# Issuing the second maxima product of a step ahead of the second piece of P times V (attention with shared keys and a gated MLP)

## The chip, the cores and the metric

One core of a Trainium2 chip runs one launch. The metric is the device time in microseconds of that launch. A profile comes from one execution, and its times count from that execution's first instruction. The engines are PE (TensorE; its weight loads are listed as PEld), DVE (VectorE), ACT (ScalarE), POOL (GpSimd) and SP, whose queue issues DMAs.

## The reference, cut to what matters

```python
mod = (silu(c) @ w_mod).reshape(1, 6, 1, 512)           # sa, ca, ga, sb, cb, gb
h = layernorm(x) * (1 + ca) + sa                        # x: 2048 x 512
q = (h @ wq) as 32 heads of 16;  k = h @ wk;  v = h @ wv   # one k and one v for all heads
p = softmax(q k^T / 4)                                  # per head 2048 x 2048
x = x + ga * ((p @ v) @ wo)
h = layernorm(x) * (1 + cb) + sb
x = x + gb * (((h @ w_gate) * (h @ w_up)) @ w_down)     # 1792 wide
```

The softmax needs, for every query and head, the maximum over the 2048 keys. The kernel forms the scores twice: once to take the maxima, and once, with the maximum subtracted by extra rows of the product, for the exponentials.

## The kernel before, in words

The 2048 queries are cut into 4 blocks of 512, the 32 heads into 8 groups of 4. A block with a head group is one of `NU` = 32 rounds, and a round has `NSTEP` = 32 steps: 16 key tiles of 128 keys (`kt`), two steps each (`p`). In one step the main loop (L1162 to L1208) issues, in this order:

- `max_half(a, 0, 2)`, the **first maxima product**: `max_mm` (L557) multiplies 128 queries of one head of a later round by 512 keys into a bank `mx` of PSUM, as four PE matmuls that each fill 32 of the 128 output partitions (`quarters`, L474), and has DVE reduce the bank to 128 maxima (L566). There are `NMX` = 2 such banks, so a product waits for the reduce of the product two before it, which is the same product of the step before.
- `pv(*who, 0)`, the **first piece of P times V** (L604): the exponentials of an earlier key tile times the values, 256 of the 512 queries, four heads. These are float32 matmuls; each shows as two PE instructions, so a piece is two sets of four.
- `qk_exp(u, kt, 0, a)`, the first **score product** (L596), four matmuls into a bank `sc`, and its exponential on ACT (L602) into a buffer `P`.
- `pv(*who, 1)`, the second piece of P times V, the other 256 queries.
- `drain_mids()`: evacuations put off from an earlier step.
- `max_half(a, 1, 2)`, the **second maxima product**, with its reduce.
- `qk_exp(u, kt, 1, a)`, the second score product and its exponential.

The maxima and score products of a step read rows 64a to 64a + 63 of the PE array, with a = `p`, and P times V reads the other 64 rows. The two row halves change places with every step. The maxima run 38 steps (`LEAD`) ahead of the exponentials; the first 38 steps of maxima are issued before the main loop, and the last 38 steps of the loop have none.

What is left of a step on PE goes to **fill work**: the query projections of later blocks, and the output projection, the gate, up and down products of the block before. A planner (`pace`, L1056; `fill_gap`, L1077) works out from counts of steps, at build time, how many units each step takes, up to `BURST` = 3. A unit (one turn of the loops in `duo`, L485) is eight matmuls, four on each row half, for two output tiles side by side. When a pair of tiles is complete, the first is evacuated at once, and the second by a function put into `mids`, which `drain_mids` (L1023) calls in the next step. On DVE that concerns the output projection (L703) and the down product (L814); the copies after the up product are ACT's (L796). The second tile's bank is given back for scores three steps after that (L507).

`max_half` (L1029) counts the maxima steps. With its second product in a step with a = 1 it also issues, once in a round (at `QPRE` = 20 of the round's 32), six DMAs on SP that load the queries of the next round (`load_q`, L546), and at the end of a round the last reduce (L572). A wait on PE stands at the head of an instruction, and the instructions behind it wait too. Schedules are written out by hand: each engine gets its instructions in the order in which this code emits them.

Of the kernel before, what the change touches and what calls it, by code (L numbers as in the profile page):

```python
# [54 lines left out]
def adaln_mqa_glu_kernel(ctx: ExitStack, tc: tile.TileContext, x_in, wq_in, wk_in, wv_in, wo_in,  # L55
# [14 lines left out]
    def ps_sc():  # L70

        spare["n"] += 1
        if spare["scores"] and spare["n"] % (NSC + 1) == 0:
            return psum.tile([128, 512], F32, name="sc", tag="spare", bufs=1)
        return psum.tile([128, 512], F32, name="sc", tag="sc", bufs=NSC)
# [398 lines left out]
    def quarters(p, left, right, start=True, stop=True):  # L474
        return [nc.tensor.matmul(p[c:c + CW, :], left[:, c:c + CW], right, start=start, stop=stop)  # L475
                for c in range(0, 128, CW)]
# [69 lines left out]
    def load_q(u):  # L546
        b, g = divmod(u, UB)
        d = qd[b, g // 2].rearrange("(h e) l n -> e h l n", e=16)
        s = sst[u % 3]
        h0 = 4 * (g % 2)  # L550
        for a in range(2):
            for r, hl in ((0, 0), (1, 0), (2, 1)):
                nc.sync.dma_start(s[64 * a + 16 * r:64 * a + 16 * r + 16, :, :], d[:, h0 + a:h0 + a + 3:2, hl, :])
# [3 lines left out]
    def max_mm(u, i, a):  # L557
        kc, r = divmod(i, 8)
        p, t = divmod(r, 4)
        s = sst[u % 3]  # L560
        if i == 0 and a == 0:
            mparts[u] = work.tile([128, 2, 2, 4, 4], F32, name="mpart")
        m = ps_mx()
        quarters(m, s[64 * a:64 * a + 48, p, t * 128:(t + 1) * 128],
                 kst[64 * a:64 * a + 48, kc * 512:(kc + 1) * 512])
        nc.vector.tensor_reduce(mparts[u][:, a, p, t, kc:kc + 1], m, axis=AX.X, op=OP.max)  # L566
# [3 lines left out]
    def max_fin(u):  # L570
        mms[u] = work.tile([128, 2, 8], F32, name="mm")
        nc.vector.tensor_reduce(mms[u], mparts[u].rearrange("p a q t k -> p a (q t) k"), axis=AX.X, op=OP.max)  # L572

    def max_rows(u):
        def f():
            p = psum.tile([16, 128], F32, name="mxt", tag="mx", bufs=NMX)
            mms[u, "p"] = p
            nc.tensor.transpose(p, mms[u].rearrange("p a c -> p (a c)"), ident)

        def g():  # L580
            p = mms[u, "p"]
            mt = [work.tile([16, 128], F16, name=f"mt{hl}") for hl in range(2)]
            nc.scalar.activation(mt[0], p, AF.Copy, scale=1.0 / 32.0)
            nc.vector.scalar_tensor_tensor(mt[1], p, 1.0 / 32.0, mt[0], op0=OP.mult, op1=OP.subtract)
            s = sst[u % 3]
            for hl in range(2):
                nc.sync.dma_start(s[48 + hl:113 + hl:64, :, :], mt[hl])
        return [(100, f, g)]
# [7 lines left out]
    def qk_exp(u, kt, p, a):  # L596
        s = sst[u % 3]
        if (u, kt, a) not in ptl:
            ptl[u, kt, a] = work.tile([128, 2, D], F32, name="P", tag="P", bufs=NP)
        t = ps_sc()  # L600
        quarters(t, kst[64 * a:64 * a + 50, kt * 128:(kt + 1) * 128], s[64 * a:64 * a + 50, p, :])
        nc.scalar.activation(ptl[u, kt, a][:, p, :], t, AF.Exp)  # L602

    def pv(u, kt, r, part=None):  # L604
        if u < 0:
            return
        if kt == 0 and not part:
            pvb[u, r] = psum.tile([128, 512], F32, name="pv", tag=("pv", "pvb")[r], bufs=1)
        ks = slice(64 * r, 64 * r + 64)
        w = 512 // PARTS  # L610
        for c in range(PARTS) if part is None else (part,):
            for j in range(4):
                p, a = divmod(j, 2)
                nc.tensor.matmul(pvb[u, r][32 * j:32 * j + 32, c * w:(c + 1) * w], vst[ks, kt, :],  # L614
                                 ptl[u, kt, a][ks, p, c * w:(c + 1) * w], start=(kt == 0 and c == 0),
                                 stop=(kt == KT - 1 and c == PARTS - 1), skip_group_check=True)
# [3 lines left out]
    def pv_lower(u):  # L620
        evt[u] = work.tile([128, BT], F32, name="ev", tag="ev", bufs=3)
        nc.scalar.activation(evt[u], pvb[u, 0], AF.Copy, scale=evs)  # L622

    def pv_out(u):
        b, g = divmod(u, UB)
        ev = evt[u]
        nc.vector.scalar_tensor_tensor(ev, pvb[u, 1], evs, ev, op0=OP.mult, op1=OP.add)  # L627
        if g % 2 == 0:
            oc[b, g // 2] = work.tile([128, BT], F32, name="oc", tag="oc", bufs=2)
            rsum[b, g // 2] = dram.tile([8, BT], F32, name=f"rs{b}_{g // 2}")  # L630
        h = 4 * (g % 2)
        for j in range(4):
            r = 16 * (h + j)
            nc.sync.dma_start(oc[b, g // 2][r:r + 16, :], ev[32 * j:32 * j + 16, :])
        nc.sync.dma_start(rsum[b, g // 2][h:h + 4, :], ev[16:128:32, :])
# [378 lines left out]
    def drain_posts():  # L1014
        todo = posts[:]
        posts.clear()
        if tick[0] is not None:
            tick[0] += 1
            todo += timers.pop(tick[0], [])
        for f in todo:  # L1020
            f()

    def drain_mids():  # L1023
        todo = mids[:]
        mids.clear()
        for f in todo:
            f()

    def max_half(a, j=0, n=1):  # L1029
        u, i = divmod(mstep[0] + j, NSTEP)  # L1030
        if a == 1 and j == n - 1:
            mstep[0] += n
        if u >= NU:
            return
        max_mm(u, i, a)
        if a == 1 and u + 1 < NU and i == (QPRE if u else QPRE0):
            load_q(u + 1)
        if i == NSTEP - 1 and a == 1:
            max_fin(u)
            (_, f, g), = max_rows(u)  # L1040
            later[mstep[0] + 1] = (f, g)
# [25 lines left out]
    def open_gate(step):  # L1067
        if not fill or (fill[0][1] == "duo" and step < cur["wait"]):
            return False
        if fill[0][1] == "duo" and NU * NSTEP - step < 2 * -(-fill[0][2][0].n // BURST) + 2:  # L1070
            return False
        gate = fill[0][0]
        if gate[0] is None:
            gate[0] = step + gate[1]
        return gate[0] <= step
# [86 lines left out]
    for u in range(NU):  # L1162
        b, g = divmod(u, UB)
        if u == 1:
            side.extend(dlist)
        for i in range(NSTEP):
            step = u * NSTEP + i
            kt, p = divmod(i, 2)
            drain_posts()
            spare["scores"] = not spare["held"] and cur["gen"] is None and not (fill and fill[0][1] == "duo" and open_gate(step))  # L1170
            a = p
            if p == 1:
                who = (u, kt - 1, 0) if kt else (u - 1, KT - 1, 0)
                if u and not kt:
                    posts.append(lambda u=u: pv_lower(u - 1))
            else:
                who = (u, kt - 2, 1) if kt > 1 else (u - 1, KT - 2 + kt, 1)
                if u and kt == 1:
                    posts.append(lambda u=u: pv_out(u - 1))
            max_half(a, 0, 2)  # L1180
            pv(*who, 0)
            qk_exp(u, kt, 0, a)
            pv(*who, 1)
            drain_mids()
            max_half(a, 1, 2)
            qk_exp(u, kt, 1, a)
            if p == 1:
                late_max()
            if fill or cur["gen"]:
                credit[0] = min(credit[0] + pace(step) / 2, 6.0)  # L1190
                if credit[0] >= 1.0:
                    fill_gap(step)
            side_step(step)
            if u > 0 and g % 2 == 0 and i in (5, 9, 15):
                if i == 5:
                    nrm = normalise((u - 1) // UB, ((u - 1) % UB) // 2)
                nrm[(5, 9, 15).index(i)]()
            if i == 16 and u > 0 and g == 0:
                ln = ln2_work(b - 1)
                due = (b + 1) * UB * NSTEP + (DUE if b < NB - 1 else LAST_DUE)  # L1200
                gate = [step + 4, 0]
                for two in twos(wo_work(b - 1)):
                    fill.append((gate, "duo", two, due))
                for gap, it in zip((TR_GAP, 0, 0, 0), ln):
                    fill.append(([None, gap], "solo", it, due))
                gate = [None, 0]
                for two in ffn_twos(b - 1):
                    fill.append((gate, "duo", two, due))  # L1208
# [72 lines left out]
```

## Time and profile before

| | |
|---|---|
| median of 3 runs | 1770.66 us (1768.67 to 1771.16) |
| the profiled execution | 1768.31 us, span 1766.5 us |
| busy: PE, DVE, ACT, POOL | 1697.3, 1438.7, 1258.7, 562.8 us |
| exponentials, L602 | 2048 of 599 ns, 1133.9 us |
| P times V, L614 | 16384 of 379 ns (they overlap), 1089.4 us |
| reduces of the maxima, L566 | 2048 of 686 ns, 1325.0 us |
| granted PE clock, mean | 0.995 |

The PE matmuls are pipelined, and their ends are modelled. A line of the timeline gives the start in microseconds, the time from the first start to the last end of the merged instructions, the engine, the line of code, the operation, output and inputs, the shapes and the count; in brackets the idle time ahead of it, and what ended that. Such a releaser is inferred from semaphores. The row of a window gives the bounds, its length, and then for the chosen instructions their busy time and count; the last three numbers are the granted PE clock, the share of the DMA engines and their GB/s.

### The profile page before, as it was taken

What the parts mean: (1) busy time and instruction counts of PE and PEld (TensorE: products, weight loads), DVE (VectorE), ACT (ScalarE), POOL (GpSimd) and SP (SyncE); (2) the same over time, 40 slices, a digit from 0 to 9 for tenths busy, and PEclk for the clock granted to TensorE, in tenths of its full rate; (3) what the DMA queues carried; (4) which work ended last, traced back from release to release, by engine and by line L of the source; (5) the groups of instructions that cost most, each with busy time, mean ns of one, the idle gap of its engine ahead of it and who ended that gap; (6) DMA issues with size and microseconds to landing.
All of it is one profiled execution on the core that took longest, in us unless ns stands there. A gap on an engine that the chain in (4) does not pass through costs nothing. (4 is left out here: it accounts for less than half of the span.)

```text
span 1766.5 us, 102784 instructions
## 1 busy us (share of the span) xinstructions
PE 1697.3 (96%) x47395; PEld 1062.5 (60%) x47395; DVE 1438.7 (81%) x2353; ACT 1258.7 (71%) x2319; POOL 562.8 (32%) x788
## 2 busy tenths in 40 slices
PE   6899999999999999999999999999999999999999
PEld 3345555555556666776656766677656666754444
DVE  7899999999998888888999888899999998922210
ACT  3478888878877777777777777777788887883110
POOL 5714454537567852210032222100032121221130
PEclk9999999999999999999999999999999999999999
DMA  5212222212222210000100000000100000001000
GB/s 195 101 31 81 61 81 63 83 42 84 77 75 68 62 27 20 6 18 24 43 23 19 13 18 14 8 18 23 49 17 19 12 19 12 14 7 41 19 0 24
DMA packets 49179, 71.09 MB, mean 40 GB/s; under 512 B 15270, under 2 KB 29418, under 8 KB 48748
## 3 DMA queue, kind: packets, MB, share of 16 engines
q1 hardware_dynamic: 47164, 64.33, 12.2%
q8 instruction: 370, 6.06, 1.5%
q14 instruction: 61, 0.50, 0.1%
q10 hardware_dynamic: 1584, 0.20, 0.1%
HBM read 51.12 MB, written 8.92 MB: 34 GB/s over the span
## 5 line engine op out<-in xcount | busy, mean ns | idle before, releaser
L566 DVE TENSOR_REDUCE mpart<-mx 128x1 f32<-128x512 f32 x2048 | 1325.0, 686 | 123.8 <-PE mx L475 46.4
L602 ACT ACTIVATE P<-sc 128x512 f32<-128x512 f32 x2048 | 1133.9, 599 | 301.0 <-PE sc L475 194.0
L614 PE MATMUL pv<-P,vst 64*32 64x256 f32 x16384 | 1089.4, 379 | 0.8 <-ACT ev L622 0.7
L475 PE MATMUL mx<-kst,sst 48*32 48x512 f16 x8192 | 815.9, 383 | 36.1 <-DVE mpart L566 28.1
L475 PE MATMUL sc<-sst,kst 50*32 50x512 f16 x8192 | 824.9, 379 | 8.4 <-ACT P L602 6.8
L614 PEld LDWEIGHTS pv<-P,vst 64*32 64x32 f32 x16384 | 486.1, 106 | 93.5 <-issue 3.2
L475 PEld LDWEIGHTS <-sst 48*32 48x32 f16 x8192 | 340.0, 90 | 295.5 <-issue 222.1
L475 PEld LDWEIGHTS <-kst 50*32 50x32 f16 x8192 | 284.1, 91 | 78.5 <-issue 50.5
L475 PE MATMUL misc<-h2T,wg 64*32 64x512 f16 x4032 | 297.5, 376 | 1.1 <-issue 1.1
L475 PE MATMUL misc<-h2T,wu 64*32 64x512 f16 x4032 | 297.6, 376 | 0.0
L797 POOL TENSOR_TENSOR gf<-gf,g 128x512 f32<-128x512 f32 x42 | 53.6, 1276 | 346.5 <-ACT gf L796 346.5
L475 PEld LDWEIGHTS <-wu 64*32 64x32 f16 x4032 | 115.8, 92 | 30.2 <-issue 1.6
L475 PEld LDWEIGHTS <-wg 64*32 64x32 f16 x4032 | 115.3, 92 | 19.1 <-issue 2.6
L475 PE MATMUL misc<-wd,glu 64*32 64x512 f16 x2688 | 121.6, 376 | 0.0
L475 PE MATMUL misc<-h,wq 64*32 64x512 f16 x1536 | 100.6, 377 | 2.1 <-ACT qf L532 2.1
L499 POOL MEMSET token<- 1x1 f32 x43 | 3.8, 88 | 283.8 <-PE misc L475 242.4
L789 ACT ACTIVATE g<-misc 128x512 f32<-128x512 f32 x56 | 33.6, 600 | 76.6 <-PE misc L522 75.5
L522 PE MATMUL misc<-wd,glu 128*128 128x512 f16 x336 | 73.2, 379 | 0.0
L475 PEld LDWEIGHTS <-glu 64*32 64x32 f16 x2688 | 60.0, 92 | 17.7 <-issue 1.3
L801 POOL TENSOR_TENSOR glu<-gf,glu 128x512 f16<-128x512 f32 x56 | 65.1, 1163 | 4.7
L799 DVE TENSOR_TENSOR gf<-misc,g 128x512 f32<-128x512 f32 x14 | 9.7, 692 | 62.9 <-PE misc L522 62.9
L627 DVE SCALAR_TENSOR_TENSOR ev<-pv,evs,ev 128x512 f32<-128x512 f32 x32 | 23.8, 743 | 44.7 <-ACT ev L622 44.7
(232 smaller groups left out, 1062.6 us busy)
## 6 DMA issues: line engine op xcount, KB each, us to landing
wsl<-in_B_w_gate_dram SPq DMA_DIRECT2D x32, 224.0 KB
wsl<-in_B_w_up_dram SPq DMA_DIRECT2D x32, 224.0 KB
wsl<-in_B_w_down_dram SPq DMA_DIRECT2D x28, 256.0 KB
sst<-qd SPq DMA_DIRECT2D x186, 32.0 KB
qd<-q SPq DMA_DIRECT2D x16, 256.0 KB
oc<-ev SPq DMA_DIRECT2D x128, 32.0 KB
rr<-ri SPq DMA_DIRECT2D x16, 256.0 KB
xl<-in_A_x_dram SPq DMA_DIRECT2D x16, 256.0 KB
```

The source lines that it names most:

```text
L475: return [nc.tensor.matmul(p[c:c + CW, :], left[:, c:c + CW], right, start=start, stop=stop) for c in range(0, 128, CW)]
L499: mark = nc.gpsimd.memset(token, 0.0)
L522: nc.tensor.matmul(p, left, right, start=i == 0, stop=i == g.n - 1)
L566: nc.vector.tensor_reduce(mparts[u][:, a, p, t, kc:kc + 1], m, axis=AX.X, op=OP.max)
L602: nc.scalar.activation(ptl[u, kt, a][:, p, :], t, AF.Exp)
L614: nc.tensor.matmul(pvb[u, r][32 * j:32 * j + 32, c * w:(c + 1) * w], vst[ks, kt, :], ptl[u, kt, a][ks, p, c * w:(c + 1) * w], start=(kt == ...
L627: nc.vector.scalar_tensor_tensor(ev, pvb[u, 1], evs, ev, op0=OP.mult, op1=OP.add)
L789: nc.scalar.activation(st["g", f], p, AF.Copy, scale=2.0 ** -45)
L797: nc.gpsimd.tensor_tensor(gf, gf, st["g", f], op=OP.mult)
L799: nc.vector.tensor_tensor(gf, p, st["g", f], op=OP.mult)
L801: nc.gpsimd.tensor_tensor(st["glu"][:, 1, f, :], gf, st["glu"][:, 0, f, :], op=OP.subtract)
```

## The change

In each step of the main loop the second maxima product, with its reduce and with the query loads and last reduce that may follow it, is issued ahead of the second piece of P times V and of the put-off evacuations. Nothing else moves.

```diff
             max_half(a, 0, 2)
             pv(*who, 0)
             qk_exp(u, kt, 0, a)
+            max_half(a, 1, 2)
             pv(*who, 1)
             drain_mids()
-            max_half(a, 1, 2)
             qk_exp(u, kt, 1, a)
             if p == 1:
                 late_max()
```

## The prediction

> **What bounds the kernel now.** I read the page first, then the waits, then cut the span into stretches, then went through single steps of the main loop in the timeline, where the change lies.
>
> ```profile
> span 1766.5 us, 102784 instructions
> ...
> PE 1697.3 (96%) x47395; PEld 1062.5 (60%) x47395; DVE 1438.7 (81%) x2353; ACT 1258.7 (71%) x2319; POOL 562.8 (32%) x788
> ...
> L566 DVE TENSOR_REDUCE mpart<-mx 128x1 f32<-128x512 f32 x2048 | 1325.0, 686 | 123.8 <-PE mx L475 46.4
> ```
>
> PE is marked busy for 96% of the span, but the loop keeps two row halves of the array at work, and "busy" means that at least one of them is. The other engine near its limit is DVE, with the 2048 reduces of L566. They sit idle for 123.8 us, of which the page gives 46.4 to the maxima product itself. The view of the waits has another part:
>
> ```profile
> DVE mpart L566 <- PE sc L475: 30.5, 157, 0.9
> PE mx L475 <- DVE mpart L566: 28.1, 75, 1.2
> ```
>
> So 157 times a reduce of a maxima tile was released when PE finished something that is not a maxima product. That is the point on which I build. The columns are the total in us, the times and the longest. The first line is idle time of the reduce, the second time in which PE stood still for a free maxima buffer.
>
> Two stretches, counted by the reduces (two in a step) and by the matmuls of the fill work (eight make a unit):
>
> ```profile
> 100.00:500.00 400.00, 363.86 (x575) 1.00 0.23 67
> 500.00:1550.00 1050.00, 902.93 (x1383) 1.00 0.09 25
> ```
>
> ```profile
> 100.00:500.00 400.00, 105.95 (x1632) 1.00 0.23 67
> 500.00:1550.00 1050.00, 510.97 (x11280) 1.00 0.09 25
> ```
>
> The first stretch has 287.5 steps of 1.391 us with 0.71 fill units each, the second 691.5 steps of 1.518 us with 2.04 units each. Together that is 979 steps, nearly the whole kernel.
>
> A step of the second stretch, from its first maxima product (M0) to the last set of P times V, and the two reduces that follow:
>
> ```profile
> 972.50 0.39 PE L475 MATMUL mx<-kst,sst 48*32 48x512 f16 x4
> 972.69 0.40 PE L614 MATMUL pv<-P,vst 64*32 64x256 f32 x4
> 972.72 0.39 PE L475 MATMUL sc<-sst,kst 50*32 50x512 f16 x4
> 972.91 0.40 PE L614 MATMUL pv<-P,vst 64*32 64x256 f32 x4
> 972.94 0.39 PE L475 MATMUL mx<-kst,sst 48*32 48x512 f16 x4
> ...
> 973.34 0.40 PE L614 MATMUL pv<-P,vst 64*32 64x256 f32 x4
> ```
>
> ```profile
> 972.96 0.69 DVE L566 TENSOR_REDUCE mpart<-mx 128x1 f32<-128x512 f32 x1 [0.50 <-PE mx L475]
> 973.84 1.51 DVE L566 TENSOR_REDUCE mpart<-mx 128x1 f32<-128x512 f32 x2 [0.19 <-PE sc L475]
> ```
>
> Maxima and score products run on one row half, P times V on the other, side by side. A piece of P times V is two sets of four, and the four sets follow each other by (973.34 - 972.69) / 3 = 0.217 us. The second maxima product (M1) starts at 972.94 and has run by 973.33. Its reduce (R1) starts at 973.84, though DVE was free at 973.65. What ends just ahead of 973.84 is the last set of P times V, at 973.74. That set stands before M1 in the program. So PE reports an instruction as done only when everything issued before it is done, although the halves overlap: R1 waits for P times V, on which it does not depend.
>
> The Trainium skill ("TensorE: Matmul & The Clock Gate", Part 3) says that matmuls start and end strictly in program order. The ends here agree (R1 0.10 us behind the P times V set, 0.51 behind its own product). The starts do not: the score product at 972.72 starts ahead of the P times V set at 972.91, which precedes it in the program.
>
> **The change part by part.** Nothing is added or removed. M1 with its reduce moves ahead of the second piece of P times V and of the waiting evacuations.
>
> *R1's release.* R1 then needs only M1 and what precedes it, 973.33 at the latest, so it can follow R0 without a gap. How close that is, a pair shows (second row below): 1.29 us for two, less 0.69 for one, is 0.60 from start to start.
>
> A step of the first stretch:
>
> ```profile
> 177.85 0.40 PE L475 MATMUL mx<-kst,sst 48*32 48x512 f16 x4
> ...
> 178.11 0.62 PE L614 MATMUL pv<-P,vst 64*32 64x256 f32 x8
> 178.45 0.40 PE L475 MATMUL mx<-kst,sst 48*32 48x512 f16 x4
> 178.54 0.40 PE L614 MATMUL pv<-P,vst 64*32 64x256 f32 x4
> ...
> 179.05 0.40 PE L475 MATMUL mx<-kst,sst 48*32 48x512 f16 x4
> ...
> 180.38 0.40 PE L475 MATMUL mx<-kst,sst 48*32 48x512 f16 x4
> ```
>
> ```profile
> 178.31 0.68 DVE L566 TENSOR_REDUCE mpart<-mx 128x1 f32<-128x512 f32 x1
> ...
> 179.04 0.69 DVE L566 TENSOR_REDUCE mpart<-mx 128x1 f32<-128x512 f32 x1
> ```
>
> Two steps take 2.53 us, 1.265 each. R0 starts 0.46 after M0, ends 0.68 later, and the next M0 goes 0.06 after that: 1.20, and it does (179.05). This loop over one maxima buffer is a floor of 1.20. The second step takes 1.33, because R1 came 0.73 after R0 instead of 0.60 and holds up what follows: it starts 0.10 after the P times V set of 178.54 had run. Released, R1 starts at 0.46 + 0.60 = 1.06 after M0, ends at 1.75, and lets the next M1 go at 1.80, so M1 stands 1.80 - T behind its own M0 if T is the step. Behind M1's start PE still has two sets on each half and the fill unit, 3 x 0.217 and some 0.02: T >= 1.80 - T + 0.67, so T = 1.235 with one unit, and the floor of 1.20 with none. Weighted with 0.71 units: 1.225. That saves 0.04 in 287.5 steps, **11.5 us**. The rest of the 1.391 is work at the turn of a head group, which stays.
>
> *The second stretch.* With three units PE needs 7 x 0.217 = 1.52 us a step and is the limit; an earlier R1 gives nothing there. With fewer, it does. An example:
>
> ```profile
> 1012.43 0.40 PE L475 MATMUL mx<-kst,sst 48*32 48x512 f16 x4
> ...
> 1013.02 0.48 PE L475 MATMUL mx<-kst,sst 48*32 48x512 f16 x4
> ...
> 1013.79 0.40 PE L475 MATMUL mx<-kst,sst 48*32 48x512 f16 x4
> ```
>
> ```profile
> 1010.67 1.46 DVE L566 TENSOR_REDUCE mpart<-mx 128x1 f32<-128x512 f32 x2
> 1012.28 1.29 DVE L566 TENSOR_REDUCE mpart<-mx 128x1 f32<-128x512 f32 x2 [0.16 <-PE sc L475]
> ```
>
> R1 of the step before starts at 1012.28, 0.15 after DVE was free (1012.13). M1 waits for its end (1012.97) and goes at 1013.02, 0.59 after its M0 instead of the 0.44 of the step at 972.50. Released, R1 gives these 0.15 back, and the next M0 comes at 1013.64. PE's own floor at 2.04 units is 6.04 x 0.217 = 1.31 against 1.518, so there is room for such gains. Their sum lies between 0 (all in three-unit steps) and 30.5 plus the short idle times that no view names, 123.8 - 46.4 - 30.5 = 46.9: 77 us. I take **25 us**, nearest to the named 30.5, less about a sixth for steps at PE's floor.
>
> *P times V behind M1's wait.* M1 waits for its buffer, and whatever is queued behind it on PE waits too. Now that is the second piece of P times V. At 178.45 this wait ended; the third set had started at 178.54 - 0.217 = 178.32, so it would come 0.13 later, together with M1, and the fourth with the second score product. The half then has its P times V done at 178.45 + 0.43 = 178.88, when the other half is done too, 0.17 ahead of the next M0, and one fill unit overshoots by 0.05. This is in the T above; it costs nothing of its own as long as R1 is early. If it is not, it is the first rival. The exponential of the second score product waits for P times V before and after; it moves with it.
>
> *The waiting evacuations* (a down or output projection's second tile) stand behind R1 on DVE and come at most one reduce, 0.69 us, later; the copies on ACT keep their place. Their bank is given back three steps later anyway: nothing (12 tiles, so 8 us if that cover were gone). *The six loads of the next queries* are issued on SP a little earlier within the step, perhaps ahead of one output store: nothing, since the code asks for them 12 steps ahead of their use.
>
> Sum: -36.5 us on the profiled 1768.31, 1731.8. The median of the runs is 2.35 higher, so **1734**.
>
> **The rivals.** *Slower: P times V is late and nothing comes back.* If R1 is not brought forward (the hold has another cause) or its gain is eaten by the next M0's completion, the 0.05 us of overshoot in each one-unit step remains, more in two-unit steps, none in three-unit steps without a wait. At 0.05 in half of 979 steps that is +25, **1795**. It decides from the point where the delay of the P times V half (0.13) exceeds its free time to the next M0 (178.76 to 179.05, less the unit: 0.07). For it: 75 listed waits of PE for a maxima buffer. Against it: R1 sits 0.10 behind the P times V set in all the steps above.
>
> *No change.* In three-unit steps PE is the limit, and if the idle time merely moves from R1 to the next R0 (46.4 us are already spent waiting for the maxima product), the time stays, 1767 to 1774: **1771**. Against it: the first stretch has no PE limit.
>
> *Much faster.* If every one of the 979 steps gets 0.10 of the 0.13 us between the present spacing (0.73) and 0.60, the gain is 98, **1673**; half of it gives 1722. Against it stand the three-unit steps.
>
> The start rule of the Trainium skill's page would have M1 start only behind all P times V sets now, and 0.43 us earlier after the change; that would lead to this last case. The rows above contradict it, and it adds nothing to that case's chance.
>
> **How the numbers follow.** Forecast (gain of 4 to 60 us, most likely 20 to 50) 0.72, much faster 0.10, no change 0.08, slower 0.10. So faster by over 0.2% (3.5 us, about what a measurement of this kernel can tell) is 0.82, within it 0.08, slower 0.10. The range goes from a gain of 70 (1700) to the middle of the no-change case (1769); beyond lie the slower case and part of the much faster one.
>
> **What would show it.** Right: the row "reduce waiting for the score product" (30.5) falls below 10; R1 follows R0 by 0.60 in steps of both stretches; the third set of P times V starts within 0.05 of M1; two steps of the first stretch take 2.40 to 2.50; three-unit steps stay at 1.52. Wrong: R1 still starts 0.10 behind some set of P times V; or R1 is early and the reduce waits longer for the first product; or PE's waits for the maxima buffer (28.1) grow by more than the reduce's idle time falls.

## The result and the profile after

| | before | after |
|---|---|---|
| median (4 runs each) | 1769.66 us | 1747.87 us |
| lowest to highest | 1766.76 to 1771.16 | 1744.23 to 1751.47 |
| the profiled execution's span | 1766.5 us | 1744.1 us |

The ratio is 0.9878, with a 95% interval of 0.9856 to 0.9899: 1.2% faster. The forecast was 1734, a gain of 36.5; 21.8 came. The changed kernel measured once more, beside later experiments, gave 1748.31, ratio 0.9879 (0.9862 to 0.9896).

The page after, its lines for the span, the engines and the reduces:

```profile
span 1744.1 us, 102800 instructions
...
PE 1674.6 (96%) x47395; PEld 988.0 (57%) x47395; DVE 1403.0 (80%) x2353; ACT 1259.0 (72%) x2319; POOL 564.1 (32%) x788
...
L566 DVE TENSOR_REDUCE mpart<-mx 128x1 f32<-128x512 f32 x2048 | 1288.1, 683 | 132.5 <-PE mx L475 120.6
```

Read the last line against that of before. DVE idles about as long as before ahead of its reduces, 132.5 us in sum against 123.8, but for another cause. The view of the waits says the same:

```profile
DVE mpart L566 <- PE mx L475: 120.6, 335, 2.1
...
PE mx L475 <- DVE mpart L566: 25.2, 61, 1.3
```

The line "reduce waiting for the score product" (30.5 us) is gone from the view. The wait for a maxima product itself has gone from 46.4 to 120.6 us; the short idle times that no view names fell from 46.9 to 11.9 (132.5 less 120.6). Idle time that only moves is no gain. One step shows it, the same as the prediction's at 972.50:

```profile
957.63 0.39 PE L475 MATMUL mx<-kst,sst 48*32 48x512 f16 x3
...
958.07 0.39 PE L475 MATMUL mx<-kst,sst 48*32 48x512 f16 x4
...
959.33 0.40 PE L475 MATMUL mx<-kst,sst 48*32 48x512 f16 x4
```

```profile
958.08 1.29 DVE L566 TENSOR_REDUCE mpart<-mx 128x1 f32<-128x512 f32 x2 [0.70 <-PE mx L475]
```

The first line has three of M0's four matmuls. R1 follows R0 by 0.60 now (1.29 less 0.69), where it came 0.88 behind. But DVE has idled 0.70 us ahead of R0, as long as ahead of both together before (0.50 and 0.19), and this step, with its three fill units, takes 1.70 us as it did before.

To compare equal work I cut both traces at the first reduces of steps 3, 288 and 985 (the row shows the bounds, the length, and busy time and count of DVE's instructions on the maxima banks; 18 of the 589 are not L566, the 1395 are all reduces). Before:

```profile
96.89:494.18 397.29, 365.32 (x589) 1.00 0.23 65
494.18:1554.09 1059.91, 911.02 (x1395) 1.00 0.10 25
```

After:

```profile
96.67:482.11 385.44, 356.52 (x589) 0.99 0.23 67
482.11:1531.78 1049.67, 883.41 (x1395) 1.00 0.10 26
```

The first 285 steps, with little fill work, save 11.85 us (1.394 to 1.352 a step), the next 697 save 10.24 (1.521 to 1.506). Together that is the whole difference of the spans, 22.4, to 0.3 us.

By the starts of the reduces in both traces, R1 stands within 0.62 us of its R0 in 45% and 34% of the steps of the two stretches before, and in 96% and 97% after.

Two steps of the first stretch after the change, with PE's sets and two of the reduces:

```profile
175.20 0.40 PE L475 MATMUL mx<-kst,sst 48*32 48x512 f16 x4
...
176.48 0.40 PE L475 MATMUL mx<-kst,sst 48*32 48x512 f16 x4
176.66 0.40 PE L614 MATMUL pv<-P,vst 64*32 64x256 f32 x4
176.70 0.40 PE L475 MATMUL sc<-sst,kst 50*32 50x512 f16 x4
176.99 0.40 PE L475 MATMUL mx<-kst,sst 48*32 48x512 f16 x4
177.00 0.42 PE L614 MATMUL pv<-P,vst 64*32 64x256 f32 x4
177.21 0.40 PE L475 MATMUL sc<-sst,kst 50*32 50x512 f16 x4
177.24 0.40 PE L614 MATMUL pv<-P,vst 64*32 64x256 f32 x4
177.42 0.44 PE L475 MATMUL misc<-h,wq 64*32 64x512 f16 x8
177.68 0.38 PE L475 MATMUL mx<-kst,sst 48*32 48x512 f16 x1
```

```profile
176.92 1.29 DVE L566 TENSOR_REDUCE mpart<-mx 128x1 f32<-128x512 f32 x2
```

The steps take 1.28 and 1.20, 2.48 for two, where before two took 2.53. The two reduces of the second one last 1.29 together, so R1 follows R0 by 0.60. The third set of P times V (177.00) now starts with M1 (176.99), whose wait has let it through, and the fourth with the second score product; both halves finish together.

The price shows in a step of three fill units in which M1 waits. Before:

```profile
994.36 0.40 PE L475 MATMUL mx<-kst,sst 48*32 48x512 f16 x4
...
994.96 0.40 PE L475 MATMUL mx<-kst,sst 48*32 48x512 f16 x4
995.05 0.40 PE L614 MATMUL pv<-P,vst 64*32 64x256 f32 x4
...
995.91 0.40 PE L475 MATMUL mx<-kst,sst 48*32 48x512 f16 x4
```

The same step after:

```profile
979.04 0.40 PE L475 MATMUL mx<-kst,sst 48*32 48x512 f16 x4
...
979.63 0.40 PE L475 MATMUL mx<-kst,sst 48*32 48x512 f16 x4
979.65 0.42 PE L614 MATMUL pv<-P,vst 64*32 64x256 f32 x4
979.89 0.40 PE L614 MATMUL pv<-P,vst 64*32 64x256 f32 x4
...
980.75 0.40 PE L475 MATMUL mx<-kst,sst 48*32 48x512 f16 x4
```

M1 goes 0.6 after M0 in both. Before, the last set of P times V starts 0.09 after M1; after the change it starts 0.26 after M1, and the next M0, behind three fill units on that half, comes 1.71 after the first instead of 1.55. The step behind it gets that back: 1.26 instead of 1.43.

### The profile page after: what moved, and what is told of

The parts are those of the page before. It is cut to its first block, busy times and chain, and to the rows that moved or that the text cites. A ratio compares the mean times of both kernels' runs of the same rounds, so it can differ in the third digit from the quotient of the medians.

```text
span 1744.1 us, 102800 instructions
## 1 busy us (share of the span) xinstructions
PE 1674.6 (96%) x47395; PEld 988.0 (57%) x47395; DVE 1403.0 (80%) x2353; ACT 1259.0 (72%) x2319; POOL 564.1 (32%) x788
## 5 line engine op out<-in xcount | busy, mean ns | idle before, releaser
L566 DVE TENSOR_REDUCE mpart<-mx 128x1 f32<-128x512 f32 x2048 | 1288.1, 683 | 132.5 <-PE mx L475 120.6
L614 PE MATMUL pv<-P,vst 64*32 64x256 f32 x16384 | 1168.4, 383 | 0.9 <-ACT ev L622 0.8
L475 PEld LDWEIGHTS <-sst 48*32 48x32 f16 x8192 | 332.2, 91 | 361.5 <-issue 263.5
L614 PEld LDWEIGHTS pv<-P,vst 64*32 64x32 f32 x16384 | 425.7, 105 | 61.3 <-issue 3.6
L475 PEld LDWEIGHTS <-kst 50*32 50x32 f16 x8192 | 295.7, 91 | 86.0 <-issue 49.6
L475 PE MATMUL misc<-wd,glu 64*32 64x512 f16 x2688 | 111.0, 376 | 0.4 <-issue 0.4
L475 PE MATMUL misc<-h,wq 64*32 64x512 f16 x1536 | 80.8, 377 | 2.4 <-ACT qf L532 2.4
L475 PEld LDWEIGHTS <-glu 64*32 64x32 f16 x2688 | 53.1, 93 | 21.1 <-issue 3.6
```

## The experiments

Theory A is the prediction's: R1 is released from P times V because PE completes in program order, and P times V pays by standing behind M1's wait. The rivals: B, the gain comes from M1 being issued earlier; C, from the evacuations' new place; D, in the second stretch there was little to gain. All diffs are against the changed kernel unless said otherwise.

**The release taken back.** The reduce is emitted behind the second piece and made to wait for its last matmul.

```diff
-            max_half(a, 1, 2)
-            pv(*who, 1)
+            max_half(a, 1, 2, late=lambda: pv(*who, 1))
...
+        behind = late() if late else None
+        red = reduce()
+        if behind is not None:
+            tc.add_manual_dep(red.ins, behind.ins.name, SYNC, reason="end of the second piece of P times V")
```

> The order of the change, but the reduce of the second maxima product is made to wait for the last matmul of the second piece of P times V as well, as PE's order of completion made it wait before. Theory A (the gain is the reduce's release from P times V; the price is that P times V now stands behind M1's wait for its buffer): the gain goes and the price stays, 1775 to 1800 us, with 0.10 us between the end of a P times V set and the reduce. Theory B (the gain comes from M1 being issued and started earlier): the time of the change stays, 1745 to 1752 us.

1828.65 us, ratio 1.0332 (1.0316 to 1.0347): 57 us slower than before and 81 slower than the change, more than expected. A step of its first stretch:

```profile
188.99 0.40 PE L475 MATMUL mx<-kst,sst 48*32 48x512 f16 x4
...
189.76 0.40 PE L475 MATMUL mx<-kst,sst 48*32 48x512 f16 x4 [0.16 <-DVE mpart L568]
189.78 0.42 PE L617 MATMUL pv<-P,vst 64*32 64x256 f32 x4
...
190.02 0.40 PE L617 MATMUL pv<-P,vst 64*32 64x256 f32 x4
...
190.45 0.40 PE L475 MATMUL mx<-kst,sst 48*32 48x512 f16 x4
```

```profile
190.48 0.69 DVE L568 TENSOR_REDUCE mpart<-mx 128x1 f32<-128x512 f32 x1 [0.17 <-PE pv L617]
```

Wait and hold close a ring: P times V waits for M1, the reduce for P times V (190.42, then 190.48), and the next M1 for the reduce. A step takes 1.46. The order of issue is that of the change, and nothing is gained: early issue alone does not bring the time, and B falls as far as that goes. (M1 starts later here, 0.77 after M0, since it waits for the reduce of the step before; an early start without the release was had in no run.) The 57 us are the price of wait and hold together, not of the wait alone: the ring needs both.

**The evacuations alone.** Against the kernel before:

```diff
             pv(*who, 1)
-            drain_mids()
             max_half(a, 1, 2)
+            drain_mids()
```

> The order of before, with the put-off evacuations alone moved behind M1 and its reduce. Theory A: nothing, 1766 to 1773 us. Theory C (what counts is that DVE takes the reduce ahead of an evacuation): a good part of the gain, 1748 to 1762 us.

1769.05 us, ratio 0.9990 (0.9980 to 0.9999): nothing beyond 0.2%. C falls.

**M1 in the middle of the second piece**, and its control.

```diff
-PARTS = 2
+PARTS = ((0, 256), (256, 384), (384, 512))
...
-            max_half(a, 1, 2)
             pv(*who, 1)
+            max_half(a, 1, 2)
+            pv(*who, 2)
             drain_mids()
```

> The second piece of P times V is cut into two of 128 queries; M1 is issued between them, so its wait holds back only the last quarter, and its reduce waits only for the quarter ahead of it. Theory A: release kept and most of the block gone, 1730 to 1742 us, if the smaller matmuls cost nothing of their own (the next run measures that). Theory D (the second stretch gives little because PE is at its floor there, not because of the block): 1745 to 1750 us.

1885.84 us, ratio 1.0635 (1.0604 to 1.0667).

> The order of before with the second piece of P times V cut in the same way, M1 behind both parts. It measures what the smaller matmuls and the 8 more weight loads of a step cost. All theories: 1766 to 1775 us if the loads stay hidden, more if they don't.

1892.12 us, ratio 1.0691 (1.0675 to 1.0707). The cut itself costs 121 us, far above the 1766 to 1775 that was expected if the loads stay hidden, so the run before it, which rests on the same cut, says little: M1 in the middle is 6 us better than M1 last. The control's two stretches, for the same steps:

```profile
97.02:506.64 409.62, 366.17 (x589) 0.99 0.22 65
506.64:1681.45 1174.81, 927.87 (x1395) 1.00 0.09 23
```

Of the 127 us by which these two are longer than before, 12 fall in the first stretch and 115 in the second, where most of the fill work lies. Whether the smaller matmuls themselves or their additional weight loads are to blame was not tried.

**The change only where P times V has time.** The steps that follow a light step and are heavy themselves keep the order of before.

```diff
-            max_half(a, 1, 2)
+            behind = taken[0] < 2 and units(step) > 1
+            if not behind:
+                max_half(a, 1, 2)
             pv(*who, 1)
             drain_mids()
+            if behind:
+                max_half(a, 1, 2)
```

> The change, except in 98 of the 1024 steps, which keep the order of before: those that follow a step with at most one fill unit (so M1 waits for its buffer) and take two or three units themselves (so the half that runs P times V has no time to spare). In the traces of before and after, such steps became 7 us longer in sum with the change, all others 29 us shorter. Theory A (the missing part of the gain was spent there, on P times V behind M1's wait): 1738 to 1744 us. Theory D (PE's floor, not the block): 1746 to 1751 us.

1743.52 us, ratio 0.9862 (0.9844 to 0.9879), 4 us better than the change.

> The opposite choice: M1 ahead of the second piece of P times V in those 98 steps alone, the order of before in all others. Theory A: the price alone, 1773 to 1780 us. Theory D: no difference or a small gain, 1764 to 1771 us.

1770.63 us against 1768.17, ratio 1.0012 (1.0002 to 1.0021). That lies in theory D's range and below A's. In this run's trace the steps so placed (93 by the count of fill matmuls) are 10.7 us longer than before in sum, and all others 10.9 shorter: what these steps lose, others get back. What is left is a cost of some 2.5 us, with 0.4 to 3.7 by the interval, and not of 7. The changed kernel and the chosen steps were then run side by side:

> The changed kernel itself, on the chip of the next run, so that the two can be compared: 1744 to 1752 us.

> The change except in the 98 chosen steps, again, beside the change itself. Theory A: 3 to 6 us faster than the run before. If the earlier 4 us were scatter: within 2 us of it.

1748.31 and 1747.59 us, ratios 0.9879 (0.9862 to 0.9896) and 0.9876 (0.9856 to 0.9896). The 4 us of the first time did not come again. The choice of steps isn't shown to be worth anything, and no run here beats the change beyond its interval.

**The same reasoning for ACT.** The first score product moves ahead of the first piece.

```diff
-            pv(*who, 0)
             qk_exp(u, kt, 0, a)
+            pv(*who, 0)
             max_half(a, 1, 2)
             pv(*who, 1)
```

> The change, and the first score product is issued ahead of the first piece of P times V as well, so its exponential no longer waits for that piece to complete. If completion in program order holds for ACT as for DVE, the exponential starts some 0.2 us earlier after its product (0.60 us after M0 instead of 0.81). ACT is not the limit, so Theory A expects little in time: 1740 to 1752 us. If ACT's waits for PE were on the path, 1725 to 1740 us.

1749.55 us, ratio 0.9890 (0.9873 to 0.9907): the time of the change. The hold was there: in the view of the waits of the change, then of this kernel, ACT's wait named after the maxima product (issued behind the score product it really waits for) all but goes. The first exponential of a step starts 0.72 us after M0 (median of the first stretch) where it was 0.81: earlier, but by 0.09 and not the 0.2 that was expected.

```profile
ACT P L602 <- PE sc L475: 208.1, 538, 1.3
...
ACT P L602 <- PE mx L475: 48.6, 88, 2.5
```

```profile
ACT P L602 <- PE sc L475: 217.6, 579, 1.2
...
ACT P L602 <- PE mx L475: 2.8, 5, 0.8
```

An engine that isn't the limit is released, and nothing follows.

**P times V still later**, behind the second score product too.

```diff
             max_half(a, 1, 2)
-            pv(*who, 1)
             drain_mids()
             qk_exp(u, kt, 1, a)
+            pv(*who, 1)
```

> The change, and the second piece of P times V is moved behind the second score product too. Neither the reduce nor an exponential waits for it then, but it stands behind the wait of the score product as well and starts 0.2 us later. Theory A: the block grows, the half with P times V ends later in each step, 1760 to 1800 us. If the releases count for more than the block: below 1748 us.

1774.92 us, ratio 1.0036 (1.0021 to 1.0051). In this order no reduce and no exponential of the step stands behind the second piece, and yet it takes 27 us more than the change. Its stretches:

```profile
96.77:487.81 391.04, 359.68 (x589) 0.99 0.23 67
487.81:1557.33 1069.52, 885.69 (x1395) 1.00 0.09 25
```

Against the change that is 6 us in the first and 20 in the second stretch. Most of the loss lies where fill work stands behind the piece, as a growing block would have it; the block itself was not measured.

**Without DVE as a limit.** Each reduce takes 128 of 512 columns, in the order of before and in that of the change.

```diff
-        nc.vector.tensor_reduce(mparts[u][:, a, p, t, kc:kc + 1], m, axis=AX.X, op=OP.max)
+        nc.vector.tensor_reduce(mparts[u][:, a, p, t, kc:kc + 1], m[:, 0:128], axis=AX.X, op=OP.max)
...
-        nc.scalar.activation(ptl[u, kt, a][:, p, :], t, AF.Exp)
+        nc.scalar.activation(ptl[u, kt, a][:, p, :], t, AF.Exp, scale=1.0 / 64.0)
```

> The order of before, but each reduce of the maxima takes 128 of its 512 columns only (so three quarters of the maxima are left out, and the exponentials are scaled by 1/64 to stay finite). DVE is then no limit, no maxima buffer is waited for, and the time of a step is what PE, ACT and the planner's spread of the fill work leave. Theory A (in the second stretch there was room for 25 us and more, lost to P times V behind M1's wait): 1.47 us a step or less in the second stretch, against 1.521 before and 1.506 with the change. Theory D (the room was never there: most of those steps are bound by PE and ACT): 1.49 us or more. In the first stretch both expect 1.2 to 1.3 us, against 1.39.

> The same short reduces in the order of the change. With no wait for a buffer in front of M1 nothing is blocked and nothing is held up, so both theories expect the time of the run before to 5 us. A longer time would mean that the new order costs PE something even without a wait.

1686.26 and 1687.45 us (two runs each), ratios 0.9534 (0.9512 to 0.9556) and 0.9541 (0.9512 to 0.9569). A step of the first stretch takes 1.245 us in both traces to 0.003. The hold is still there in the first run and gone in the second: 301.2 us of the reduces' idle time are put down to a score product, 592 times, and none in the order of the change. Their second stretches:

```profile
444.94:1471.65 1026.71, 399.80 (x1394) 1.00 0.10 26
```

```profile
446.19:1470.19 1024.00, 403.53 (x1394) 1.00 0.10 26
```

With next to no wait (PE stands 4.2 and 4.5 us for a maxima buffer, 28.1 before) the two orders are equal: the new order costs PE nothing that these runs can tell. And with DVE almost out of the way the 697 steps still take 1026.71 us, 1.473 each, between what A and D expected. So the short reduces gain 1059.91 - 1026.71 = 33 us in that stretch (36 in the order of the change), which is about all the room that the maxima had there. The change got 10 of it.

## Why the prediction was right in its way and too large

*What bounds the kernel, and the release:* right. R1 follows R0 by 0.60 in both stretches, and the wait for the foreign product is gone. The trace's record of PE's semaphore shows the hold at PE itself: in the prediction's step at 972.50, M0 is signalled 0.05 us after its own end, and M1 0.49 after its own and 0.07 after the end of the last set of P times V. That the gain hangs on this release, and not on the order of issue or the evacuations alone, is shown by the first two experiments. Of the signs that the prediction set down, the third set's start (0.01 behind M1) and the 2.48 for two steps came too; one sign of being wrong came as well, that R1 is early and the reduce waits longer for the first product.

*The first stretch:* right in mechanism; that the size agrees so closely, 11.85 us against 11.5, is partly luck. T = 1.235 with one unit was forecast, and the two steps above took 1.28 and 1.20 (mean 1.24). Over all steps that are shorter than 1.45 us in both traces, by the starts of the first products, the 95 without fill work go from 1.26 to 1.20 as forecast, and the 122 with one unit from 1.26 to 1.25 only. That is 7.4 us. The rest comes from the other 68, longer steps, which the forecast counted with the same 0.04.

*The second stretch:* the term that failed, 25 us forecast and 10.2 measured. Two parts of its working were wrong.

The first is the way from idle time to gain: the named idle time, 30.5, was taken nearly whole. Summed over the 697 steps, R1 came 84.6 us nearer to its R0 (509.0 to 424.5), more than the forecast counted on; but the next R0 came 74.3 us later behind R1 (550.9 to 625.2), and only the difference is a gain. The prediction named that move under its rival of no change, and gave it to that case alone instead of to a part of the forecast.

The second is the room, taken from means: "PE's own floor at 2.04 units is 6.04 x 0.217 = 1.31 against 1.518". The 697 steps have very different loads. By the fill matmuls between one M1 and the next, and the starts of the first products:

| fill units | steps | before, us | after, us | change in sum, us | short reduces, us |
|---|---|---|---|---|---|
| 0 | 106 | 1.50 | 1.45 | -5.3 | 1.22 |
| 1 | 52 | 1.30 | 1.26 | -2.1 | 1.19 |
| 2 | 251 | 1.40 | 1.38 | -4.9 | 1.36 |
| 3 | 288 | 1.67 | 1.68 | +2.1 | 1.72 |

That three-unit steps gain nothing was forecast and holds, but they take 1.67 in the mean and not the 1.52 of the prediction, and no less with the short reduces. Even a count step by step, with the prediction's own floors (1.20, 1.235, and 6 and 7 times 0.217), gives 1.37 a step. The short reduces show 1.473; the 25 us would have been three quarters of the room that this leaves. What holds the heavy steps above 1.52 was not found. That one step's spare time can't serve the next with two maxima buffers may be part of it; no run shows it.

*P times V behind M1's wait:* "it costs nothing of its own as long as R1 is early" holds in the first stretch, and nearly so in the second. By the starts of the first products, the 93 steps that follow a step of at most one unit and take two or three themselves became 7 us longer in sum (the pair of steps above is not of these, since it follows a step of three units, but M1 waits in it too); run alone, the new order in the 98 steps so chosen costs 2.5. That is too small to explain the 15 us that are missing. The price of the slower rival was set too low: with the release taken back, so that wait and hold close their ring, it was 57 us where 25 was written.

*Evacuations and query loads at nothing:* right for the evacuations, measured by themselves. The loads were not tried alone.

*Program order:* of the rule of the Trainium skill ("TensorE: Matmul & The Clock Gate", Part 3) the ends agree, as far as the starts of the reduces and exponentials show them, in the traces of before and of the experiments. The starts do not, and the last case, to which they would have led, is not near.

## What to carry to other kernels

When two streams run side by side on the row halves of PE, the order of issue decides whom a consumer waits for: put the product whose result is awaited ahead of the long work that nobody awaits. Read that from the releaser's name: an engine that is released by a product it doesn't read may be held by order. Then ask what the released engine will wait for next, since here most of what it won went into the wait for the next product. And measure the room, by a run in which that engine is no limit: a mean over light and heavy steps promised 0.2 us a step, a sum of floors step by step 0.15, where 0.05 was to be had.

## What the runs showed of the hardware that was not expected

Cutting a 256-column float32 product for P times V into two of 128 columns, with eight more weight loads a step, cost 121 us of 1771 where the number of columns stayed the same.

The page's busy time of the reduces fell from 1325.0 to 1288.1 us with the same work. A reduce that finds its data ready follows the one ahead of it by 0.60 us, though each is recorded with 0.68 to 0.69, so that their records overlap, and the busy time counts an overlap once. A falling busy time is here a sign of closer packing, not of less work.
